# Windowed attention with sinks and channel mix: the sinks' v rows by GpSimd transfers, sink scores of two units in one group, casts off GpSimd, and new instruction orders

## The chip, the cores and the metric

The kernel runs on one core of one Trainium2 chip. The metric is the device time of one execution in microseconds, the median of a few runs. The core's engines are named as the profile names them: PE (matrix multiply), PEld (its weight loads), DVE (vector), ACT (scalar, activations), POOL (GpSimd) and SP (the queue that issues most DMAs).

## The reference, cut to what matters

Attention over 4 batches, 8 heads, 768 positions and a head size of 64, in which a position sees the 128 latest positions and the first four (the sinks); then a channel mix (FFN) over the 512 joined head columns, in which each row is blended with the row before it.

```
keep = (pos[None, :] < n_sink) | ((rel >= 0) & (rel < window))   # n_sink 4, window 128
scores = np.where(keep, scale * q @ k.T, -1e9)
a = exp(scores - max);  a = a / (sum(a) + 1e-9)
x = (a @ v) as [batch, seq, 512]
x_prev = x one position later, zeros first
xk = mu_k * x + (1 - mu_k) * x_prev
xr = mu_r * x + (1 - mu_r) * x_prev
k = maximum(xk @ w_k, 0)                 # 512 -> 1024
v = (k * k) @ w_v                        # 1024 -> 512
out = sigmoid(xr @ w_r) * v
```

## The kernel before

**Tiles.** The 768 positions of a batch are cut into three *units* of 256 positions, 12 units in all, numbered `u`; batch `b, T = divmod(u, 3)`. A unit is taken through four stages, each written as a function that records operations:

- `load` and `prepare(u)`: k, q and v come by SP's DMAs in fp32 (`ks`, `qs`, `vs`, two transfers of 256 KB each, lines 307, 317 and 337). They are cast to bf16 (`kb`, `qb`, `vb`; lines 536, 543, 646) by ACT, DVE or POOL. k and q are turned so that the head dimension lies on the partitions: for early units by PE transposes (L576) and a copy out of PSUM (`kt`, `qt`; L589), for later ones by a DMA transpose (L562).
- `attend(u)`: scores `sc` in PSUM (L721; two heads side by side, each in 64 rows of the PE array: *row-tiled*), `e = exp(sc)` on ACT (L775), a 0/1 mask on DVE (L789; units 0 and 1 have instead a bias that PE adds to the scores, L728, made by POOL in a tile that the profile calls `ob`), value matmuls `vb, e` (L808), and division by the sum of weights, which is a 65th column (reciprocal L822, product `x` L825).
- `mix(u)`: x is transposed (PE L849 and a copy L858, or a DMA transpose L869), the difference with the position before (`td`, L877) and the two blends `xk`, `xr` (L888) are made on DVE.
- `ffn(u)`: keys (L939), relu and square (`rl` L949 or L953, `kk` L963 or L967), gate (L979) with its tanh (`th` L985), product (L997, L909), `(th + 1) * product` on DVE (L1006, L919), store (L1013, L924). The weights `wk`, `wr`, `wv` come in fp32 and are cast once (L501, L505, L507).

**The sinks.** Units with T = 1 and T = 2 do not hold the first four positions of their batch among their own keys, so these come apart. `ksink` holds the four sink keys of all heads (copied by POOL from the turned k of the batch's first unit, L670), `vsink` their value rows. Per unit there is a group of four *column-tiled* matmuls for the sink scores (32 columns each, L696), one `es = exp` on ACT (L703), and sink value matmuls in 64 rows (L763) that start the sums to which L808 adds. `vsink` is made per batch by PE and DVE: a matmul with the 0/1 matrix `spread` puts the four v rows (from `vb` of the batch's first unit) onto the partitions where `es` has their weights, into a PSUM bank (L676); DVE multiplies them there with `hmask`, which keeps a head's rows and clears the others (L680).

**What sets the order.** Nothing is scheduled at run time. The functions record 1,052 operations in a `Plan`; `ORDER` is the list of their numbers in the order in which they are emitted, `CHOICE` says which engine takes an operation that several can do, and `SLOTS` which buffer of a pool each tile gets. Negative entries of `ORDER` are warm matmuls on zeros (L1018), which only keep PE working. Each engine executes its own instructions in this order and waits on semaphores for the others; four PSUM banks (`bank`) and two pairs (`sc`) are shared by all PE work. `JOINT` lists the batches in which the sink scores of the units T = 1 and T = 2 are one group; before, it is empty. Such a batch's third unit is prepared ahead of `attend` of its second (line 1027), since the group needs the q of both.

Of the kernel before, what the change touches and what calls it, by code (L numbers as in the profile page):

```python
# [18 lines left out]
    92: "ACT", 93: "ACT", 94: "ACT", 95: "ACT", 97: "ACT", 100: "ACT", 102: "DVE", 105: "DVE",  # L19
    110: "DVE", 111: "DVE", 114: "ACT", 115: "DVE", 139: "POOL", 142: "POOL", 145: "POOL", 148:  # L20
    "DVE", 150: "DVE", 151: "ACT", 152: "ACT", 154: "DVE", 161: "DVE", 191: "DVE", 193: "DVE",
    194: "DVE", 197: "DVE", 199: "DVE", 200: "DVE", 203: "DVE", 204: "DVE", 213: "DVE", 230:
    "ACT", 234: "ACT", 273: "DVE", 276: "DVE", 279: "DVE", 282: "DVE", 285: "ACT", 286: "ACT",
    298: "DVE", 306: "DVE", 315: "ACT", 354: "DVE", 364: "ACT", 365: "DVE", 367: "DVE", 383:
    "ACT", 387: "ACT", 436: "DVE", 439: "DVE", 444: "DVE", 445: "DVE", 467: "ACT", 475: "ACT",
    514: "DVE", 516: "DVE", 521: "DVE", 524: "ACT", 525: "ACT", 546: "ACT", 550: "ACT", 554:
    "ACT", 558: "ACT", 595: "DVE", 598: "DVE", 603: "ACT", 604: "ACT", 606: "DVE", 634: "ACT",
    681: "DVE", 682: "DVE", 691: "DVE", 700: "ACT", 704: "ACT", 708: "ACT", 755: "DVE", 759:
    "DVE", 760: "ACT", 772: "DVE", 781: "ACT", 785: "ACT", 789: "ACT", 834: "DVE", 836: "DVE",
    837: "DVE", 853: "ACT", 856: "DVE", 857: "ACT", 860: "DVE", 861: "ACT", 904: "DVE", 906:  # L30
    "DVE", 910: "DVE", 912: "DVE", 913: "DVE", 929: "ACT", 933: "ACT", 940: "DVE", 941: "ACT",
    994: "DVE", 995: "ACT", 999: "ACT", 1003: "ACT", 1007: "ACT", 1022: "DVE", 1026: "DVE",
    1034: "DVE", 1035: "ACT",
# [13 lines left out]
JOINT = ()  # L47
# [138 lines left out]
def kernel(  # L186
# [19 lines left out]
    NS = 4  # L206
# [199 lines left out]
    def fill_later():  # L406
        for t in ksink + vsink:
            nc.vector.memset(t, 0.0)
# [666 lines left out]
```

## Time and profile before

| what | value |
|---|---|
| timed runs | 165.51, 165.54 and 166.27 us, median 165.54 us |
| profiled execution, first to last instruction | 164.3 us |
| PE busy / DVE busy / ACT busy / POOL busy | 158.4 / 145.4 / 131.2 / 13.5 us |
| weight loads (PEld) busy | 102.6 us |
| matmuls | 1603 |
| moved by DMA | 34.60 MB, a mean of 211 GB/s |
| HBM read / written | 24.12 / 6.29 MB |
| mean granted TensorE clock | 0.999 |

The profile is of one execution; of its time only the span from the first to the last instruction is known, 164.3 us. How to read its rows: a group of instructions stands with its line, engine, operation, what it writes and reads (`out<-in`, buffer numbers left out), its count, its busy time in us and the mean of one in ns, then the idle time of the engine just before it and who ended it. The windows give, for each stretch, the busy time of each engine. The list of waits says who waited for whom, in us, how often, and the longest. The chain follows the last instruction back to what released it, step by step. Busy times count overlapping instructions of one engine once; the mean of one instruction reaches into the next, so steps of the chain are shorter than the means.

### The profile page before, as it was taken

Reading aid. Unit: us, or ns where it says so; the run is one execution under the profiler, and the core shown is the slowest. Engines: PE = TensorE matmul, PEld = TensorE weight load, DVE = VectorE, ACT = ScalarE, POOL = GpSimd, SP = SyncE. Lnnn points to the kernel's source line nnn. Section 1 sums busy time; section 2 is a strip of 40 time slices with the busy share of each in tenths; the row PEclk is TensorE's granted clock in tenths of the full one; section 3 lists DMA queues with packets and bytes.
Section 4 is the critical chain, followed back from the end, with each engine's and each line's share of the span. In section 5 each row is a group of like instructions: output and inputs, shape, how many; then the busy total and the mean of one; then the engine's idle time right before and its main releaser. Section 6 shows DMA issues by size and latency. Waiting matters only on the chain.

```text
span 164.3 us, 4195 instructions
## 1 busy us (share of the span) xinstructions
PE 158.4 (96%) x1603; PEld 102.6 (62%) x1603; DVE 145.4 (89%) x381; ACT 131.2 (80%) x218; POOL 13.5 (8%) x38
## 2 busy tenths in 40 slices
PE   6999889999999999999999999999999999999992
PEld 2455568866467587577566775856575765664851
DVE  5259999999999999989999999999999999789752
ACT  3277999999999999999999999997668759163240
POOL 6409300010000000060000000000000000000000
PEclk9999999999999999999999999999999999999999
DMA  4999999999969896999999887986996955077743
GB/s 120 247 305 311 348 335 355 301 354 210 228 154 270 135 240 148 234 198 167 224 216 157 188 156 163 235 146 150 199 123 136 362 149 200 0 90 297 262 185 128
DMA packets 79042, 34.60 MB, mean 211 GB/s; under 512 B 67112, under 2 KB 73520, under 8 KB 79024
## 3 DMA queue, kind: packets, MB, share of 16 engines
q1 hardware_dynamic: 79008, 34.35, 86.3%
q8 instruction: 12, 0.20, 0.6%
q14 instruction: 6, 0.05, 0.1%
q10 hardware_dynamic: 16, 0.00, 0.0%
HBM read 24.12 MB, written 6.29 MB: 185 GB/s over the span
## 4 chain that ended last, share of the span: by engine, by line
PE 79%; ACT 8%; SPq 4%; DMA 3%; issue 2%; DVE 1%; POOL 1%; DVEq 0%; ACTq 0%; POOLq 0%
PE bank L997 23%; PE bank L939 23%; PE bank L979 12%; PE bank L808 6%; PE sc L721 6%; SPq L337 3%; DMA qs<-in_q_dram 3%; PE bank L576 2%; ACT e L775 2%; PE bank L849 2%; ACT rl L949 1%; PE bank L763 1%; ACT qt L589 1%; PE bank L909 1%; PE bank L1018 1%
## 5 line engine op out<-in xcount | busy, mean ns | idle before, releaser
L775 ACT ACTIVATE e<-sc 128x1024 bf16<-128x1024 f32 (+1 forms) x48 | 46.1, 994 | 1.8 <-PE sc L721 1.7
L939 PE MATMUL bank<-xk,wk_sb 128*128 128x256 bf16 x384 | 47.1, 273 | 0.0
L997 PE MATMUL bank<-wv_h,kk 128*128 128x512 bf16 x184 | 43.1, 379 | 0.1
L939 PEld LDWEIGHTS <-wk_sb 128*128 128x128 bf16 x384 | 36.4, 98 | 7.4 <-issue 0.4
L949 ACT ACTIVATE rl<-bank 128x512 bf16<-128x512 f32 x40 | 24.2, 625 | 8.6 <-PE bank L939 7.1
L997 PEld LDWEIGHTS <-kk 128*128 128x128 bf16 x184 | 17.1, 98 | 17.8 <-issue 0.4
L789 DVE TENSOR_TENSOR e<-e,mask 128x1024 bf16<-128x1024 bf16 (+1 forms) x40 | 25.4, 642 | 0.7 <-ACT e L775 0.5
L979 PE MATMUL bank<-wr_sb,xr 128*128 128x512 bf16 x96 | 23.7, 379 | 0.0
L888 DVE SCALAR_TENSOR_TENSOR xk<-td,mu_all,xt 128x256 bf16<-128x256 bf16 x48 | 22.4, 483 | 0.3
L888 DVE SCALAR_TENSOR_TENSOR xr<-td,mu_all,xt 128x256 bf16<-128x256 bf16 x48 | 22.1, 475 | 0.2
L967 ACT ACTIVATE kk<-rl 128x512 bf16<-128x512 bf16 x29 | 18.3, 664 | 4.2 <-DVE rl L953 4.0
L985 ACT ACTIVATE th<-bank 128x512 f32<-128x512 f32 x24 | 15.1, 646 | 5.7 <-PE bank L979 5.7
L825 DVE TENSOR_TENSOR x<-bank,rec 128x256 bf16<-128x256 f32 x48 | 19.2, 416 | 0.4
L808 PE MATMUL bank<-vb,e 128*128 128x65 bf16 x352 | 16.6, 194 | 0.0
L1006 DVE SCALAR_TENSOR_TENSOR w<-th,bank 128x512 f32<-128x512 f32 x19 | 13.0, 682 | 3.6 <-issue 1.8
L808 PEld LDWEIGHTS <-e 128*128 128x128 bf16 x352 | 13.6, 97 | 3.5
L979 PEld LDWEIGHTS <-xr 128*128 128x128 bf16 x96 | 8.8, 98 | 8.6 <-issue 0.2
L721 PE MATMUL sc<-qt,kt 64*128 64x128 bf16 (+1 forms) x256 | 13.9, 238 | 0.0
L721 PEld LDWEIGHTS <-kt 64*128 64x128 bf16 x256 | 8.9, 94 | 5.7 <-issue 3.1
L1018 PE MATMUL bank<-warm 128*128 128x512 bf16 x30 | 10.6, 484 | 1.1 <-DVE warm L1038 1.1
L877 DVE TENSOR_TENSOR td<-xt 128x512 bf16<-128x512 bf16 x24 | 10.3, 428 | 0.7 <-ACT xt L858 0.5
L589 ACT COPY qt<-bank 128x512 bf16<-128x512 bf16 x15 | 9.4, 643 | 1.0 <-PE bank L576 1.0
(74 smaller groups left out, 161.7 us busy)
## 6 DMA issues: line engine op xcount, KB each, us to landing
ks<-in_k_dram SPq DMA_DIRECT2D x24, 256.0 KB, 4.7
qs<-in_q_dram SPq DMA_DIRECT2D x24, 256.0 KB, 4.4
vs<-in_v_dram SPq DMA_DIRECT2D x24, 256.0 KB, 4.4
out_dram<-w SPq DMA_DIRECT2D x19, 256.0 KB, 2.7
w<-in_moe_w_k_dram SPq DMA_DIRECT2D x2, 1024.0 KB, 10.4
w<-in_moe_w_v_dram SPq DMA_DIRECT2D x2, 1024.0 KB, 9.3
w<-in_moe_w_r_dram SPq DMA_DIRECT2D x1, 1024.0 KB, 9.7
out_dram<-ob SPq DMA_DIRECT2D x4, 256.0 KB, 2.6
```

The source lines that it names most:

```text
L721: nc.tensor.matmul(out=sc[:, a, o0:o1], lhsT=lhs[rows], rhs=rhs[rows], start=u not in BIAS, stop=True, skip_group_check=u in BIAS)
L775: nc.scalar.activation(out=buf[ek][:, :, lo:], in_=buf[sck][:, :, lo:], func=AF.Exp, scale=scale)
L789: nc.vector.tensor_tensor(out=at, in0=at, in1=m, op=ALU.mult)
L808: nc.tensor.matmul(out=o[:, g, a, :], lhsT=e[:, a, e0:e0 + 128], rhs=rhs, start=(T == 0 and i == 0), stop=(i == len(blocks) - 1), skip_gro ...
L825: P.op("DVE", dve(256), lambda ok=ok, rk=rk, c=c: nc.vector.tensor_tensor(out=buf["x", u][:, :, 128 * c:128 * c + 128].rearrange("p g (a d ...
L888: nc.vector.scalar_tensor_tensor(out=buf[key][:, c, :], in0=buf[tk][:, i, :], scalar=mu[w][:, c:c + 1], in1=xt[:, c, t0 - 1:t0 + 255], op0 ...
L939: nc.tensor.matmul(out=ps[:, i, :], lhsT=wk_sb[:, c, 128 * f:128 * f + 128], rhs=xk[:, c, :], start=(c == 0), stop=(c == NC - 1), skip_gro ...
L949: nc.scalar.activation(out=buf[rk], in_=buf[psk].rearrange("p (i t) -> p i t", i=2), func=AF.Relu)
L967: nc.scalar.activation(out=buf["kk", u][:, 2 * f2:2 * f2 + 2, :], in_=buf[rk], func=AF.Square)
L979: nc.tensor.matmul(out=buf[psk], lhsT=buf["xr", u][:, c, 128 * g:128 * g + 128], rhs=wr_sb[:, c, :], start=(c == 0), stop=(c == NC - 1))
L985: P.op("ACT", act(512), lambda psk=psk, tk=tk: nc.scalar.activation(out=buf[tk], in_=buf[psk], func=AF.Tanh, scale=0.5), rank + 4 + g, tak ...
L997: nc.tensor.matmul(out=buf[psk], rhs=wv_h[:, f, :], lhsT=buf["kk", u][:, f, 128 * g:128 * g + 128], start=(f == 0), stop=(f == NF - 1))
```

## The change

- The four sink rows of v no longer go through PE. A tile `vstage` (128 partitions, 4 batches, 64 columns, fp32) is cleared by DVE at the start. For each of the four sinks POOL issues one transfer that reads that position's row of every head and batch from HBM into every 16th partition of `vstage` (8 partitions, 4 x 64 values). They are POOL's first DMAs in this kernel; all others stay on SP and ACT.
- `vsink` is now `vstage * hmask`, from SBUF. POOL or DVE can do it; the new `CHOICE` gives all four to DVE. The matmul with `spread`, `spread` itself and the PSUM bank are gone. The partitions where a head's sink weights lie change with it (a step of 16 in place of 4, in `ksink`, `hmask` and `vstage` alike).
- `JOINT` names all four batches: the sink scores of the two units of a batch are one group of eight matmuls, with one `es` of 512 columns in place of two of 256.
- POOL has no casts any more (before: one of `qb`, two of `kb`).
- `ORDER`, `CHOICE` and `SLOTS` are new throughout. Counted in the two programs: on ACT four weight casts fewer (two of `wk`, one `wr`, one `wv`), four `es` fewer and of twice the size, nine `qb` casts more and two `kb` casts fewer, two `vb` casts and two `rl` more; on DVE the counterparts, four weight casts more, eight `qb` and two `vb` casts fewer, four `kb` casts more, two `rl` fewer. PE has 1599 matmuls, 30 of them warm ones as before.

The diff, cut to its core (the tables to a line each):

```diff
 CHOICE = {
-    92: "ACT", 93: "ACT", 94: "ACT", 95: "ACT", 97: "ACT", 100: "ACT", 102: "DVE", 105: "DVE",
+    95: "DVE", 96: "ACT", 97: "DVE", 98: "ACT", 99: "DVE", 100: "DVE", 101: "DVE", 102: "DVE",
...
-JOINT = ()
+JOINT = (0, 1, 2, 3)
...
 ORDER = (
-    80, 81, 78, 82, 87, 83, 84, 77, -1, -2, -3, -4, -1, -2, 90, 0, 1, 79, 102, 108, -2, -3, -4,
+    80, 82, 83, -1, -2, -3, -4, -1, 121, 77, 88, 86, 81, 79, 2, 3, 108, 89, 0, 1, 4, 114, -2, -3,
...
-    spread = tile1([128, 128], BF16, "spread")
...
+    vstage = tile1([128, B, D], FP32, "vstage")
...
-        for t in ksink + vsink:
+        for t in ksink + vsink + [vstage]:
             nc.vector.memset(t, 0.0)
...
             m = hmask[:, a::2, :]
-            keep(m, -4 * a, [[-32, NP], [0, D + 1]], 1, m)
-            keep(m, 3 + 4 * a, [[32, NP], [0, D + 1]], -1, m)
+            keep(m, -16 * a, [[-32, NP], [0, D + 1]], 1, m)
+            keep(m, 3 + 16 * a, [[32, NP], [0, D + 1]], -1, m)
...
+    for i in range(NS):
+        P.op("POOL", 1000.0, lambda i=i: nc.gpsimd.dma_start(
+            out=vstage[i::16], in_=v[:, :, i, :].rearrange("b h d -> h b d")), -50,
+            service=60.0, descs=32, reads=["stage0"], writes=[("vstage", i)])
...
-                nc.gpsimd.tensor_copy(out=kz[rows, :, 4 * a:4 * a + NS],
+                nc.gpsimd.tensor_copy(out=kz[rows, :, 16 * a:16 * a + NS],
                                       in_=first(rows))
...
-        psk = ("vsp", b)
-        P.op("PE", 220.0, lambda: nc.tensor.matmul(
-            out=buf[psk].rearrange("p (h d) -> p h d", h=H), lhsT=spread,
-            rhs=buf["vb", u][:, 0, :, 0:D], start=True, stop=True), rank + 4, lag=PE_LAG,
-            take=[("bank", psk)], hold=[("vb", u)], reads=["spread", ("vb", u, 0)], writes=[psk])
-        P.op("DVE", dve(512), lambda: nc.vector.tensor_tensor(
-            out=vsink[b % 2][:, :, 0:D], op=ALU.mult, in1=hmask[:, :, 0:D],
-            in0=buf[psk].rearrange("p (h d) -> p h d", h=H)), rank + 4, hold=[psk],
-            reads=[psk, "hmask", "sinks"], writes=[("vsink", b % 2)])
+        def sink_values(engine):
+            return lambda: engine.tensor_tensor(
+                out=vsink[b % 2][:, :, 0:D], op=ALU.mult, in1=hmask[:, :, 0:D],
+                in0=vstage[:, b, :].unsqueeze(1).to_broadcast([128, H, D]))
+
+        P.op("POOL", 1250.0, sink_values(nc.gpsimd), rank + 4, port=True,
+             alts={"POOL": (1250.0, sink_values(nc.gpsimd), True),
+                   "DVE": (dve(512), sink_values(nc.vector), True)},
+             reads=[("vstage", i) for i in range(NS)] + ["hmask", "sinks"],
+             writes=[("vsink", b % 2)])
```

The places of the order on which the prediction rests stand in it, as rows of the built programs: the first `vsink` on DVE, SP's first loads, and the start of POOL's queue. There `L` numbers are those of the kernel that is shown; most lines of the changed kernel lie some 10 further on.

More of the change, by code (lines that the diff above doesn't have):

```diff
@@ L18 @@
 CHOICE = {
-    92: "ACT", 93: "ACT", 94: "ACT", 95: "ACT", 97: "ACT", 100: "ACT", 102: "DVE", 105: "DVE",
[L20 to L30, printed above, removed]
@@ L31 @@
-    "DVE", 910: "DVE", 912: "DVE", 913: "DVE", 929: "ACT", 933: "ACT", 940: "DVE", 941: "ACT",
-    994: "DVE", 995: "ACT", 999: "ACT", 1003: "ACT", 1007: "ACT", 1022: "DVE", 1026: "DVE",
-    1034: "DVE", 1035: "ACT",
+    95: "DVE", 96: "ACT", 97: "DVE", 98: "ACT", 99: "DVE", 100: "DVE", 101: "DVE", 102: "DVE",
+    103: "DVE", 104: "DVE", 105: "DVE", 107: "ACT", 108: "ACT", 110: "DVE", 111: "DVE", 113:
+    "ACT", 114: "ACT", 116: "DVE", 117: "DVE", 118: "DVE", 120: "DVE", 141: "DVE", 143: "DVE",
@@ new lines @@
+    144: "DVE", 146: "ACT", 147: "DVE", 149: "ACT", 150: "ACT", 152: "ACT", 153: "DVE", 154:
+    "DVE", 156: "DVE", 163: "DVE", 169: "DVE", 171: "ACT", 172: "DVE", 174: "DVE", 175: "ACT",
+    177: "ACT", 178: "ACT", 180: "ACT", 181: "DVE", 182: "ACT", 208: "ACT", 215: "DVE", 223:
+    "ACT", 224: "DVE", 227: "ACT", 228: "ACT", 231: "ACT", 232: "DVE", 235: "ACT", 236: "ACT",
+    273: "DVE", 275: "ACT", 276: "DVE", 278: "ACT", 279: "DVE", 281: "ACT", 282: "ACT", 284:
+    "ACT", 285: "DVE", 286: "ACT", 288: "DVE", 290: "DVE", 297: "DVE", 305: "ACT", 306: "ACT",
@@ new lines @@
+    309: "ACT", 310: "DVE", 313: "ACT", 314: "ACT", 317: "ACT", 318: "ACT", 353: "ACT", 355:
+    "ACT", 357: "ACT", 358: "DVE", 360: "ACT", 362: "ACT", 363: "ACT", 364: "ACT", 366: "ACT",
+    373: "ACT", 381: "ACT", 382: "DVE", 385: "ACT", 386: "ACT", 389: "ACT", 390: "DVE", 393:
+    "ACT", 394: "ACT", 407: "DVE", 409: "DVE", 411: "ACT", 412: "DVE", 414: "ACT", 416: "ACT",
+    417: "ACT", 418: "ACT", 446: "DVE", 453: "ACT", 461: "ACT", 462: "ACT", 465: "ACT", 466:
+    "DVE", 469: "ACT", 470: "ACT", 473: "ACT", 474: "ACT", 511: "DVE", 513: "ACT", 515: "ACT",
@@ new lines @@
+    516: "DVE", 518: "DVE", 520: "ACT", 521: "DVE", 522: "ACT", 524: "DVE", 526: "ACT", 533:
+    "ACT", 541: "DVE", 542: "ACT", 545: "ACT", 546: "ACT", 549: "ACT", 550: "DVE", 553: "ACT",
+    554: "DVE", 589: "DVE", 591: "ACT", 593: "ACT", 594: "DVE", 596: "DVE", 598: "ACT", 599:
+    "ACT", 600: "DVE", 602: "ACT", 609: "ACT", 617: "ACT", 618: "ACT", 621: "ACT", 622: "DVE",
+    625: "ACT", 626: "DVE", 629: "DVE", 630: "DVE", 643: "ACT", 645: "ACT", 647: "ACT", 649:
+    "ACT", 651: "DVE", 652: "DVE", 680: "ACT", 687: "DVE", 695: "ACT", 696: "ACT", 699: "ACT",
@@ new lines @@
+    700: "ACT", 703: "ACT", 704: "ACT", 707: "ACT", 708: "ACT", 745: "ACT", 747: "ACT", 749:
+    "ACT", 751: "ACT", 753: "ACT", 754: "DVE", 756: "DVE", 758: "ACT", 765: "DVE", 773: "ACT",
+    774: "ACT", 777: "ACT", 778: "ACT", 781: "ACT", 782: "ACT", 785: "ACT", 786: "ACT", 821:
+    "ACT", 823: "ACT", 825: "ACT", 827: "ACT", 829: "ACT", 830: "ACT", 845: "ACT", 846: "DVE",
+    849: "ACT", 850: "DVE", 853: "ACT", 854: "ACT", 857: "DVE", 858: "DVE", 871: "ACT", 873:
+    "ACT", 875: "DVE", 877: "ACT", 879: "ACT", 880: "ACT", 921: "ACT", 922: "ACT", 925: "ACT",
@@ L34 @@
+    926: "DVE", 929: "ACT", 930: "ACT", 933: "DVE", 934: "DVE", 985: "ACT", 986: "ACT", 989:
+    "ACT", 990: "DVE", 993: "ACT", 994: "ACT", 997: "ACT", 998: "ACT", 1013: "ACT", 1014: "DVE",
+    1017: "DVE", 1018: "ACT", 1021: "ACT", 1022: "ACT", 1025: "DVE", 1026: "DVE",
 }
@@ L400, in fill @@
     def fill():
-        for t, value in ((ones, 1.0), (spread, 0.0), (hmask, 1.0)):
+        for t, value in ((ones, 1.0), (hmask, 1.0)):
             nc.vector.memset(t, value)
@@ L414 @@
     const_op("DVE", 500.0, fill, ["ones0"], rank=-80)
-    const_op("DVE", 1800.0, fill_later, ["sinks0", "ones", "edges"], rank=-79)
+    const_op("DVE", 1800.0, fill_later, ["sinks0", "stage0", "ones", "edges"], rank=-79)
     def keep(out, base, pattern, multiplier, in_=ones, fill=0.0):
@@ L446, in make_bias1 @@
         window_mask(early.bitcast(BF16)[:, 384:640], warm[:, 0:128], LOW)
-    def make_spread():
-        for a in range(2):
-            nc.gpsimd.tensor_copy(
-                out=spread[0:NS, :].rearrange("p (c w) -> p c w", w=32)[:, :, 4 * a:4 * a + NS],
-                in_=ident[0:NS, 0:NS].unsqueeze(1).to_broadcast([NS, NP, NS]))
     def make_hmask():
@@ L479 @@
     const_op("POOL", 1250.0, make_mask0, ["mask0"], ["ones0"], rank=-55)
-    const_op("POOL", 200.0, make_spread, ["spread"], ["ident", "ones0"], rank=-54)
     const_op("POOL", 1400.0, make_hmask, ["hmask"], ["ones0"], rank=-53)
```

155 rows, old and new, of tables (ORDER, SLOTS) are left out of this document.

## The prediction

> **What bounds the kernel now.** I read the page's busy shares and slices first, then the windows by stage, then the waits, then the chain.
>
> ```profile
> span 164.3 us, 4195 instructions
> PE 158.4 (96%) x1603; PEld 102.6 (62%) x1603; DVE 145.4 (89%) x381; ACT 131.2 (80%) x218; POOL 13.5 (8%) x38
> ...
> PE   6999889999999999999999999999999999999992
> ...
> DVE  5259999999999999989999999999999999789752
> ACT  3277999999999999999999999997668759163240
> ...
> GB/s 120 247 305 311 348 335 355 301 354 210 228 154 270 135 240 148 234 198 167 224 216 157 188 156 163 235 146 150 199 123 136 362 149 200 0 90 297 262 185 128
> ...
> PE 79%; ACT 8%; SPq 4%; DMA 3%; issue 2%; DVE 1%; POOL 1%; DVEq 0%; ACTq 0%; POOLq 0%
> ```
>
> PE is busy in 96% of the span and carries 79% of the chain that ended last. A busy PE is not proof of a full PE, so the windows have to say in which stage something else could hold it (columns: PE, PEld, DVE, ACT and POOL busy, clock, DMA share, GB/s).
>
> ```profile
> 20.00:30.00 10.00, 9.50 (x132) 7.47 (x129) 9.83 (x28) 10.00 (x15) 0.00 (x0) 1.00 1.11 342
> ...
> 60.00:70.00 10.00, 10.00 (x109) 7.01 (x106) 9.71 (x26) 10.00 (x18) 0.00 (x0) 1.00 0.89 194
> ...
> 100.00:110.00 10.00, 10.00 (x121) 6.76 (x119) 9.66 (x26) 10.00 (x18) 0.00 (x0) 1.00 0.97 177
> 110.00:120.00 10.00, 10.00 (x94) 6.25 (x93) 9.93 (x29) 7.66 (x14) 0.00 (x0) 1.00 1.07 158
> ```
>
> From 20 to 110 us three engines are full at once: PE, ACT at 10.00 of 10 and DVE above 9.6. ACT has room only after 110 us (7.66 of 10). So PE sets the time, but work given to ACT or DVE before 110 us has no idle time to fall into. The waits say where PE still stands still:
>
> ```profile
> POOL qb L543 <- DMA qs<-in_q_dram: 6.7, 1, 6.7
> ...
> PE bank L696 <- ACT qt L589: 0.5, 1, 0.5
> PE bank L576 <- DVE vsink L680: 0.5, 1, 0.5
> PE bank L576 <- POOL qb L543: 0.3, 1, 0.3
> ```
>
> The first row is POOL's own wait for a load; the three of PE, 1.3 us together, all lie in the head of the kernel, the one on POOL at 13.5 us behind that load, the other two in PE's timeline (start, us, what, in brackets the idle time ahead and who ended it):
>
> ```profile
> 18.06 0.38 PE L576 MATMUL bank<-ident,qb 128*128 128x128 bf16 x4 [0.46 <-DVE vsink L680]
> ...
> 21.84 0.29 PE L696 MATMUL bank<-qt,ksink 128*32 128x256 bf16 x4 [0.50 <-ACT qt L589]
> ```
>
> The list of waits has no other of PE but for its very first instruction: after the head PE loses almost nothing to data. The profiled execution has a span of 164.3 us; the median of the timed runs, 165.5 us, is 1.2 us more, which lies outside the first and last instruction and which the change does not touch. I make the sum on the profiled execution and add the 1.2 us.
>
> **The change part by part.** Spread matmuls and mode changes, from the chain (start, us, what):
>
> ```profile
> 16.93 0.23 PE bank L676
> ...
> 38.59 0.35 PE bank L808 x8
> ...
> 39.16 0.24 PE bank L808 x8
> ...
> 60.24 0.59 ACT xt L858
> ...
> 64.64 0.50 ACT kb L536
> ...
> 67.06 0.28 ACT es L703
> ...
> 70.27 0.49 ACT rl L949
> ...
> 72.52 0.50 ACT qt L589
> ```
>
> The matmul with `spread` (L676) takes 0.23 us of PE and there are four, one a batch: taken away, 0.9 us less on the engine that sets the end. The same eight value matmuls (L808) take 0.35 us right behind row-tiled ones and 0.24 us elsewhere: PE pays 0.11 us each time it changes between full, row-tiled (scores, sink values) and column-tiled (sink scores) matmuls. Putting the sink scores of two units in one group halves those groups from eight to four, but I count in the two orders of PE how often its mode changes: 66 times before, 67 now, because more score groups stand apart from their sink values. So this part gives PE nothing, +0.1 us. All other matmuls are the same in number and size, the 30 warm ones included.
>
> The vector product for `vsink` moves from PSUM to the staged rows. On DVE, at the first batch, before and then after (names are tiles, `bank` is PSUM):
>
> ```order
> L822 RECIPROCAL rec_104<-bank_65 128x4
> L680 TENSOR_TENSOR vsink_153<-bank_64,hmask 128x8x64
> L825 TENSOR_TENSOR x_107<-bank_65,rec_104 128x2x128
> L543 CAST qb_84<-qs_72 128x2x4x64
> L888 SCALAR_TENSOR_TENSOR xr_117<-td_110,mu_all,xt_155 128x256
> ```
>
> ```order
> L869 COPY xt_155<-bank_64 128x2x256
> L599 COPY qt_91<-bank_66 128x2x256
> L686 TENSOR_TENSOR vsink_152<-vstage,hmask 128x8x64
> L888 TENSOR_TENSOR td_111<-xt_155 128x512
> L656 CAST vb_136<-vs_74 128x8x64
> ```
>
> Before, the product held `bank_64`, which PE's next transposes needed; that is PE's wait of 0.5 us on `vsink`. Now no bank is held, so I take that 0.5 us off. Its cost could lie anywhere between a cast's 0.42 us and a weight cast's 0.68 us (rows below); I leave it as it was, the same operation on as many elements.
>
> SP's loads of the first three units, before and after (`ks_67`, `qs_70` are unit 0's, `ks_68`, `qs_71`, `vs_74` unit 1's, `qs_72`, `ks_69` unit 2's):
>
> ```order
> L307 DMA vs_73<-in_v_dram 128x8x64 x2
> L337 DMA ks_68<-in_k_dram 64x4x256
> L337 DMA qs_71<-in_q_dram 64x4x256 x2
> L337 DMA ks_68<-in_k_dram 64x4x256
> L307 DMA vs_74<-in_v_dram 128x8x64
> L337 DMA qs_72<-in_q_dram 64x4x256 x2
> ```
>
> ```order
> L319 DMA vs_73<-in_v_dram 128x8x64 x2
> L349 DMA ks_68<-in_k_dram 64x4x256 x2
> L349 DMA qs_71<-in_q_dram 64x4x256 x2
> L349 DMA qs_72<-in_q_dram 64x4x256 x2
> L349 DMA ks_69<-in_k_dram 64x4x256 x2
> L319 DMA vs_74<-in_v_dram 128x8x64 x2
> ```
>
> The bytes ahead of the weights are the same, but unit 1's q moves one transfer of 256 KB back, 0.8 us at the 305 to 348 GB/s of those slices. Its cast leaves POOL:
>
> ```profile
> 5.65 0.32 POOL L451 COPY spread<-ident 4x16 bf16<-4x16 bf16 x2
> ...
> 12.64 0.86 POOL L543 CAST qb<-qs 128x512 bf16<-128x512 f32 x1 [6.67 <-DMA qs<-in_q_dram]
> ...
> 13.48 0.62 POOL L543 CAST kb<-ks 128x512 bf16<-128x512 f32 x1
> ...
> 14.05 1.00 POOL L418 TENSOR_SCALAR_AFFINE_SELECT mask<-ones 128x128 bf16<-128x128 bf16 x2
> ...
> 15.07 1.03 PE L728 MATMUL sc<-ob,ident 128*128 128x512 bf16 x4
> ...
> 15.74 0.55 POOL L470 COPY vsink<-hmask 128x8 bf16<-128x8 bf16 x2
> ```
>
> The cast took 0.86 us on POOL. On DVE it takes 0.42 (row below), so 0.4 of the 0.8 us comes back and PE's wait of 0.3 us on that q stays; the third wait, 0.5 us for ACT's `qt` ahead of sink scores, I halve, since the joint group now stands behind both score groups but needs unit 2's q too. What is late next in the head is that q. Head: 0.5 + 0 + 0.25 = 0.75 us less; 0 to 1.3 are the bounds.
>
> What ACT and DVE get is counted from the two orders and priced by the groups (mean ns of one):
>
> ```profile
> L949 ACT ACTIVATE rl<-bank 128x512 bf16<-128x512 f32 x40 | 24.2, 625 | 8.6 <-PE bank L939 7.1 <-ACT kk L967 0.9 <-ACT rl L949 0.2
> ...
> L536 ACT CAST kb<-ks 128x512 bf16<-128x512 f32 x10 | 6.6, 655 | 0.0
> ...
> L543 DVE CAST qb<-qs 128x512 bf16<-128x512 f32 x11 | 4.6, 416 | 2.3 <-DMA qs<-in_q_dram 2.3
> ...
> L501 ACT ACTIVATE wk_sb<-w 128x1024 bf16<-128x1024 f32 x4 | 4.2, 1092 | 0.0
> ...
> L703 ACT ACTIVATE es<-bank 128x256 bf16<-128x256 f32 x8 | 3.3, 407 | 0.0
> ...
> L953 DVE TENSOR_SCALAR rl<-bank 128x512 bf16<-128x512 f32 x8 | 5.5, 685 | 1.5 <-PE bank L939 1.5
> ...
> L543 ACT CAST qb<-qs 128x512 bf16<-128x512 f32 x4 | 2.7, 768 | 0.0
> ...
> L507 DVE CAST wr_sb<-w 128x1024 bf16<-128x1024 f32 x1 | 0.7, 682 | 0.0
> ```
>
> ACT: eight `es` of 0.41 become four of the size of `rl`, 0.63 (-0.8 us); four weight casts go (-4.4); two more `rl` (+1.25); six more `qb` casts at L543 (+4.6) and three more of `qb`, `kb` and `vb` in sum (+2.0): +2.7 us. Means overlap their successors; by the chain's steps (0.50 for a cast, 0.49 `rl`, 0.28 `es`, and 0.95 for a weight cast, its mean less the same 0.14) it is -0.3 - 3.8 + 1.0 + 4.5 = +1.4 us. DVE: six casts fewer (-2.5), four weight casts more (+2.7), two `rl` fewer (-1.4), a memset of `vstage` in its idle head (+0.3): -0.9 us. DVE's relief is behind a full PE and I count it as nothing. ACT's +1.4 to +2.7 us is hidden where PE has FFN matmuls to run; where ACT carries the chain (8% of the span, 13 us, nearly all of it between the first and the last of the chain's ACT rows above, 60 to 73 us) it is not. 13 of the 90 full microseconds is 15%, 0.2 to 0.4 us, and I take 0.5 us to leave something for waits of the new order that no row can show.
>
> POOL's queue, from its masks on, before and after (`ob` is the bias that PE adds to units 0 and 1, its first three rows and memset for unit 0, the next two for unit 1):
>
> ```order
> L418 AFFINE_SELECT hmask<-hmask 128x4x65 x4
> L418 AFFINE_SELECT ob_134<-warm 128x128 x3
> L434 MEMSET ob_134 4x256
> L418 AFFINE_SELECT ob_134<-warm 128x128 x2
> L451 COPY spread<-ident 4x4x4 x2
> L543 CAST qb_83<-qs_71 128x2x4x64
> ```
>
> ```order
> L431 AFFINE_SELECT hmask<-hmask 128x4x65 x4
> L491 DMA vstage<-in_v_dram 8x4x64 x3
> L476 COPY vsink_152<-hmask 128x8
> L476 COPY vsink_153<-hmask 128x8
> L491 DMA vstage<-in_v_dram 8x4x64
> L431 AFFINE_SELECT ob_134<-warm 128x128 x2
> ```
>
> Four transfers now stand ahead of unit 1's bias. Before, `hmask` and both biases were done at 5.65 us; now the window mask (1.00), the `vsink` copies (0.55) and four transfers come first, so the bias is ready at 7.2 us plus four times what a transfer holds POOL. PE used it at 15.07 us. If it is wanted then again, a transfer may take 1.97 us. No row shows a transfer on POOL. The nearest below is a POOL cast, 0.62 to 0.86 us; the nearest above is the landing of an SP store, if POOL were held until then:
>
> ```profile
> out_dram<-w SPq DMA_DIRECT2D x19, 256.0 KB, 2.7
> ```
>
> I take 0.9 us, near the POOL rows, because an issue is an instruction of the queue and not a landing: ready at 10.8 us, nothing lost. The range keeps both ends: 0 and, at 2.7 us each, 18.0 us, 2.9 us late. The longer of the two POOL casts ran beside a DVE cast from 12.62 us on, the shorter one later. The Trainium skill, "SBUF — State Buffer", section "SBUF: two separate sides", says why that could be: GpSimd and some DVE instructions, fp32 copies among them, take an exclusive lock on a shared port pair, and a transfer issued from GpSimd then waits since its descriptors can't be written. The trace agrees as far as 0.62 against 0.86 us goes; the page's own example, some 3.1 us for a transfer beside a DVE copy, would as an estimate put the bias at 19.6 us, 4.5 us late.
>
> The sum: 165.5 - 0.9 + 0.1 - 0.75 + 0.5 = 164.5 us.
>
> **The rivals.** First, the forecast: PE stays full, the four matmuls and about half of the head's waits are saved; 164.5 us, its own range 163.2 (all 1.3 us and a little of DVE's relief) to 164.9. Chance 0.50.
>
> Second, the head gives its part back: unit 2's q and k must now be cast, transposed and copied before the joint sink scores, on an ACT that is full from 20 us on, and unit 1's v comes four transfers later (3.3 us). The three waits then go to other places in the same head, and new ones take half of what the four matmuls gave: 165.5 - 0.9 + 0.1 + 0.5 = 165.2 us. For it speaks that ACT's `qt` copy ended one of the waits already; against it that fewer casts stand between load and transpose. Chance 0.26.
>
> Third, on the other side: ACT becomes the bound. Its extra work lies before 110 us, where its windows read 10.00 of 10, and PE runs out of FFN matmuls as it did between 60 and 73 us. It decides from about 2.4 us of unhidden ACT work on; at the full 2.7 us: 165.5 - 0.9 + 0.1 - 0.75 + 2.7 = 166.7 us. Against it: only 13 us of the chain are ACT's, and it can catch up after 110 us. Chance 0.14.
>
> Fourth, POOL: the transfers hold it for more than 1.97 us each, PE waits for the bias of unit 1, and with a full PE behind it all of that stays. At 2.7 us each: 164.5 + 2.9 = 167.4 us. For it: the 0.86 us cast beside DVE. Against it: a third of the 1.97 us is what POOL's casts take at their quickest. Chance 0.10.
>
> **How the numbers follow.** 164.5 us is the likeliest. A measurement of this kernel can tell about 0.5% (0.8 us) from no change, so faster means below 164.7 and slower above 166.4 us. Most of the forecast's 0.50 lies below 164.7 and a little of it not: faster 0.48. The rest of it, the second case and the mild half of what ACT could cost: same 0.30. ACT at its full price and POOL: slower 0.22. The range, 163.2 to 166.6 us, holds the first two cases and the milder part of the third; outside are POOL (0.10), ACT at its worst (0.06) and a little below.
>
> **What would show it.** Right: the wait of PE's transposes on `vsink` gone; PE's busy time lower by about 1 us, with ACT still at 10.00 of 10 between 20 and 110 us; POOL done with unit 1's bias near 11 us. Wrong: a PE wait on POOL `ob` near 15 us (fourth case); ACT with a share of the chain well over 8% (third); PE waits in the head that still sum to more than 1 us (second).

## The result, and the profile after

The changed kernel took 166.83 us (median of 16 runs, 165.78 to 168.5), the kernel before, timed beside it, 165.91 us (median of 16, 165.51 to 166.85). The ratio is 1.0052, with a 95% interval of 1.0028 to 1.0075: slower by half a per cent, where 164.5 us and a gain had been forecast. In a second measurement it was 1.0074 (1.0047 to 1.0101). Averages below leave out the few executions that lay over 1.5% above their kernel's fastest, three of the changed kernel's 27 among them (with these three its mean span is 165.08 us).

Each run lists its time and its span, first to last instruction. Over all runs of the study:

| | runs | mean span, us | spread of the spans (standard deviation) | time less span |
|---|---|---|---|---|
| before | 99 | 164.34 ± 0.04 | 0.41 | 1.86 |
| after | 24 | 164.92 ± 0.14 | 0.69 | 2.12 |

The changed kernel was measured ahead of the experiments and beside the first set of them, not beside the later two; before, measured beside each of the three sets, has mean spans of 164.23, 164.39 and 164.30 us, so a difference of 0.1 or 0.2 us between sets says nothing.

The loss of 0.84 us has two parts: 0.26 us outside the span and 0.58 us in it, together with a wider spread. The profiled execution of the changed kernel shows nothing of the second part: at 163.7 us it is the fastest of its 24. Its page (the first line of part 1, two DMA queues of part 3, the chain's shares):

```profile
span 163.7 us, 4180 instructions
PE 157.6 (96%) x1599; PEld 101.6 (62%) x1599; DVE 144.6 (88%) x377; ACT 132.5 (81%) x221; POOL 10.8 (7%) x37
...
q1 hardware_dynamic: 79008, 34.35, 91.1%
...
q0 software_dynamic: 128, 0.03, 0.1%
...
PE 84%; ACT 5%; DVE 3%; DMA 3%; issue 1%; SPq 1%; DVEq 0%; ACTq 0%
```

PE's busy time fell by 0.8 us (158.4 before) and ACT's rose by 1.3 (131.2). The queue of software transfers, q0, is new: the 128 packets that GpSimd starts. PE's list of waits, whole:

```profile
PE bank L1029 <- DVE warm L1049: 1.1, 1, 1.1
PE bank L586 <- ACT qb L553: 0.5, 1, 0.5
PE bank L774 <- ACT es L714: 0.4, 1, 0.4
PE sc L732 <- ACT kt L599: 0.2, 1, 0.2
PE sc L732 <- ACT e L786: 0.2, 1, 0.2
```

The first row is the very first instruction, as before. The wait on `vsink` is gone, and so are the other two; four others stand in their place, and their sum is 1.3 us as it was. The windows over the head and over the stretch from there to 160 us, of before and then of after (PE, PEld, DVE, ACT, POOL busy, clock, DMA share, GB/s):

```profile
0.00:24.00 24.00, 21.48 (x217) 11.69 (x218) 16.75 (x54) 16.31 (x26) 9.86 (x32) 1.00 0.94 277
24.00:160.00 136.00, 135.85 (x1380) 90.20 (x1380) 127.65 (x326) 114.88 (x193) 3.62 (x6) 1.00 0.87 202
```

```profile
0.00:24.00 24.00, 21.30 (x227) 11.63 (x228) 18.22 (x57) 16.41 (x26) 9.32 (x31) 1.00 0.96 276
24.00:160.00 136.00, 135.80 (x1374) 89.78 (x1371) 125.79 (x319) 116.05 (x197) 1.52 (x6) 1.00 0.93 203
```

Between 24 and 160 us PE is full in both. In the head PE stands idle for 2.5 us before and 2.7 us after. Two of its new waits, in its timeline:

```profile
6.00 0.62 PE L586 MATMUL bank<-ident,qb 128*128 128x128 bf16 x8 [0.47 <-ACT qb L553]
...
21.48 0.29 PE L774 MATMUL bank<-vsink,es 64*128 64x130 bf16 x4 [0.36 <-ACT es L714]
```

The first stands ahead of unit 0's transposes: both halves of unit 0's q are now cast by ACT, one behind the other (4.80 and 5.33 us), where before the two halves of the first load, k, were cast side by side on ACT and DVE (4.84 and 4.86 us). The second is the wait for the joint `es`. POOL's queue, which one rival feared:

```profile
5.41 1.76 POOL L491 DMA_DIRECT2D vstage<-in_v_dram  x3
7.17 0.36 POOL L476 COPY vsink<-hmask 128x8 bf16<-128x8 bf16 x2
7.43 0.70 POOL L491 DMA_DIRECT2D vstage<-in_v_dram  x1
8.14 0.72 POOL L431 TENSOR_SCALAR_AFFINE_SELECT ob<-warm 128x128 bf16<-128x128 bf16 x2
```

A transfer holds POOL for 0.6 to 0.7 us here, and the bias of unit 1 is done at 8.9 us.

### The profile page after: what moved, and what is told of

The parts are those of the page before. It is cut to its first block, busy times and chain, and to the rows that moved or that the text cites. A ratio compares the mean times of both kernels' runs of the same rounds, so it can differ in the third digit from the quotient of the medians.

```text
span 163.7 us, 4180 instructions
## 1 busy us (share of the span) xinstructions
PE 157.6 (96%) x1599; PEld 101.6 (62%) x1599; DVE 144.6 (88%) x377; ACT 132.5 (81%) x221; POOL 10.8 (7%) x37
## 4 chain that ended last, share of the span: by engine, by line
PE 84%; ACT 5%; DVE 3%; DMA 3%; issue 1%; SPq 1%; DVEq 0%; ACTq 0%
PE bank L950 26%; PE bank L1008 24%; PE bank L990 13%; PE bank L819 7%; PE sc L732 6%; DMA ks<-in_k_dram 3%; ACT e L786 3%; PE bank L860 2%; PE bank L586 2%; PE bank L774 2%; SPq L349 1%; PE bank L920 1%; DVE x L836 1%; ACT kt L599 1%; PE bank L707 1%
## 5 line engine op out<-in xcount | busy, mean ns | idle before, releaser
L786 ACT ACTIVATE e<-sc 128x1024 bf16<-128x1024 f32 (+1 forms) x48 | 45.5, 970 | 1.8 <-PE sc L732 1.7
L950 PE MATMUL bank<-xk,wk_sb 128*128 128x256 bf16 x384 | 46.4, 273 | 0.0
L1008 PE MATMUL bank<-wv_h,kk 128*128 128x512 bf16 x184 | 44.0, 379 | 0.0
L960 ACT ACTIVATE rl<-bank 128x512 bf16<-128x512 f32 x42 | 24.8, 613 | 10.9 <-PE bank L950 10.8
L1008 PEld LDWEIGHTS <-kk 128*128 128x128 bf16 x184 | 17.1, 98 | 16.8
L899 DVE SCALAR_TENSOR_TENSOR xk<-td,mu_all,xt 128x256 bf16<-128x256 bf16 x48 | 21.7, 478 | 0.0
L996 ACT ACTIVATE th<-bank 128x512 f32<-128x512 f32 x24 | 14.5, 614 | 4.3 <-PE bank L990 3.9
L888 DVE TENSOR_TENSOR td<-xt 128x512 bf16<-128x512 bf16 x24 | 9.8, 417 | 1.6 <-DMA xt<-x 1.6
L1029 PE MATMUL bank<-warm 128*128 128x512 bf16 x30 | 9.6, 427 | 1.1 <-DVE warm L1049 1.1
L833 DVE RECIPROCAL rec<-bank 128x4 f32<-128x4 f32 x48 | 7.8, 174 | 2.0 <-PE bank L819 1.5
```

What stands on the lines that cost most here:

```text
L786: nc.scalar.activation(out=buf[ek][:, :, lo:], in_=buf[sck][:, :, lo:], func=AF.Exp, scale=scale)
L899: nc.vector.scalar_tensor_tensor(out=buf[key][:, c, :], in0=buf[tk][:, i, :], scalar=mu[w][:, c:c + 1], in1=xt[:, c, t0 - 1:t0 + 255], op0 ...
L950: nc.tensor.matmul(out=ps[:, i, :], lhsT=wk_sb[:, c, 128 * f:128 * f + 128], rhs=xk[:, c, :], start=(c == 0), stop=(c == NC - 1), skip_gro ...
L960: nc.scalar.activation(out=buf[rk], in_=buf[psk].rearrange("p (i t) -> p i t", i=2), func=AF.Relu)
L996: P.op("ACT", act(512), lambda psk=psk, tk=tk: nc.scalar.activation(out=buf[tk], in_=buf[psk], func=AF.Tanh, scale=0.5), rank + 4 + g, tak ...
L1008: nc.tensor.matmul(out=buf[psk], rhs=wv_h[:, f, :], lhsT=buf["kk", u][:, f, 128 * g:128 * g + 128], start=(f == 0), stop=(f == NF - 1))
```

## The experiments

**The transfers.** The first theory (A) was that transfers started by GpSimd cost time outside the span. The rivals: the order itself is slower (B), or the transfers disturb the span (C). Four kernels; the first is the changed kernel unaltered.

> The changed kernel once more, for its profile, its spans and a second set of times. The theory (A): the transfers that GpSimd starts itself cost a fixed time ahead of the first or behind the last instruction, so the run's time is again about 2.1 us longer than its span, where before's is 1.2 us longer. The rival (B): the new order is itself slower or more easily disturbed, so that the span, 163.7 us in the first profile, comes out near before's 164.3 or above. The other rival (C): the four transfers disturb other transfers inside the span, in some executions more than in others; then the span varies by over 1 us and the wait rows of VectorE, ScalarE or TensorE on DMAs do so with it.

Measured: 167.44 us (median of 11), mean span 165.17, 2.14 us outside it.

```
-        P.op("POOL", 1000.0, lambda i=i: nc.gpsimd.dma_start(
+        P.op("POOL", 1000.0, lambda i=i: nc.scalar.dma_start(
```

> The changed kernel, with the four transfers into vstage started by ScalarE's queue in place of GpSimd's; nothing else differs. Theory A: the time outside the span falls from 2.1 us to about 1.2, and the kernel runs in about 165.9 us where the changed one takes 166.8, against 165.9 before: 0.995 of the changed kernel. Rival B: no difference to the changed kernel over 0.3 us, and 2.1 us outside the span stays. Rival C: the time outside stays at 2.1 us, and the span varies less from run to run.

Measured: 167.97 us, 1.0105 of before (1.0075 to 1.0134); outside the span 1.73 us, a fall as A has it, though of 0.4 us and not of 0.9, and a mean span of 166.1 us. Set against the first profile of the changed kernel, its profile is 1.4 us late at 24 us and 2.4 us at the end, so more than half of what it loses lies in the head. There ACT issues the transfers between its casts, and SP, which waits for earlier loads to land as well (1.8 us for `ks`), now waits for one of these too (SP's waits, then ACT's timeline):

```profile
SPq L349 <- DMA vstage<-in_v_dram: 1.5, 1, 1.5
```

```profile
4.85 0.69 ACTq L491 DMA_DIRECT2D vstage<-in_v_dram  x1
5.58 0.62 ACT L553 CAST qb<-qs 128x512 bf16<-128x512 f32 x1
5.59 1.27 ACTq L491 DMA_DIRECT2D vstage<-in_v_dram  x2
```

```
-        P.op("POOL", 1000.0, lambda i=i: nc.gpsimd.dma_start(
-            out=vstage[i::16], in_=v[:, :, i, :].rearrange("b h d -> h b d")), -50,
+        P.op("POOL", 1000.0, lambda: None, -50,
```

> The changed kernel without the four transfers into vstage: the sinks' v rows stay zero, so the sinks' part of the numerator is left out of the output; every other instruction is there. Theory A: about 1.2 us outside the span and about 165.9 us in all, as with the transfers started by ScalarE. Rival B: as slow as the changed kernel, 166.8 us. Rival C: the span is shorter in its slower runs than the changed kernel's, with 2.1 us outside.

Measured: 166.66 us, 1.0038 of before (1.0015 to 1.0061); outside the span 1.70 us, mean span 164.99 ± 0.20. The span is no shorter without the transfers (C falls), and half of the loss or more stays without them: 1.0038 of before, where the changed kernel has 1.0074 beside it and 1.0052 in the first measurement (B, in part).

In the next kernel these lines stand at the end of `make_spread`, where GpSimd is idle:

```
+        for i in range(NS):
+            nc.gpsimd.dma_start(out=vstage[i::16], in_=v[:, :, i, :].rearrange("b h d -> h b d"))
```

> The kernel before, with the four transfers added on GpSimd's queue at a place where GpSimd stands idle (6 to 12.6 us); the tile that they fill is read by nothing, and nothing waits for them. Theory A: the span stays at 164.3 us, the time outside it rises from 1.2 to about 2.1 us, and the kernel takes about 0.85 us longer than before, a ratio of 1.005. Rival B: the ratio is 1.000 within 0.002, since the order is before's. Rival C: the span itself grows by some tenths of a us, and its runs spread more than before's.

Measured: 166.53 us, 1.0025 of before (1.0008 to 1.0042); outside the span 2.08 us instead of 1.86, mean span 164.53 ± 0.17 instead of 164.34. A later run of the same with `range(1)`:

> The kernel before with one of the four transfers on GpSimd's queue (the other three left out), its tile read by nothing. With four the time outside the span rose from 1.87 to 2.08 us. If that is a price of the program (it has such transfers or has none) it comes to 2.08 again; if it is a price of each transfer, to 1.92.

Measured: 1.98 us outside the span, ratio 1.0006 (0.9986 to 1.0026). So one transfer costs 0.12 us outside the span and four cost 0.22: neither a price of the program alone nor an equal one of each. A is right, and small: about a quarter of a microsecond of the loss. In the new order the same four transfers are worth 0.42 us (2.12 against 1.70); that order without them has 0.16 us less outside the span than before has, and no run shows why. (The 1.2 us that I call before's time outside the span in these expectations, and 1.9 later, are the same thing; the 1.2 was wrong, see below.)

**Where long executions lose.** The kernel without transfers happened to be profiled in a span of 166.6 us, 2.9 us over the first profile of the changed kernel, with the same instructions in the same order but for those four. Set against that profile, PE's k-th weight load is level at 6 us, 0.8 us late at 23 us, 1.4 at 48 and, within a few matmuls at 90 us, 3.0 us late; then nothing more is lost. PE waits there on ACT. The same stretch of ACT's timeline, first in the fast profile of the changed kernel, then in the long one:

```profile
83.11 0.59 ACT L599 COPY qt<-bank 128x512 bf16<-128x512 bf16 x1 [0.18 <-PE bank L586]
83.59 1.14 ACT L546 CAST kb<-ks 128x512 bf16<-128x512 f32 x2
84.63 1.94 ACT L786 ACTIVATE e<-sc 128x1024 bf16<-128x1024 f32 x2
```

```profile
84.53 0.59 ACT L598 COPY qt<-bank 128x512 bf16<-128x512 bf16 x1 [0.18 <-PE bank L585]
85.02 0.62 ACT L545 CAST kb<-ks 128x512 bf16<-128x512 f32 x1
87.49 0.62 ACT L545 CAST kb<-ks 128x512 bf16<-128x512 f32 x1 [1.85 <-DMA ks<-in_k_dram]
88.02 1.93 ACT L785 ACTIVATE e<-sc 128x1024 bf16<-128x1024 f32 x2
```

The chain of the long execution runs through this load, from its issue on (start, us, what):

```profile
82.80 4.67 DMA ks<-in_k_dram
87.47 0.02 issue
87.49 0.03 ACT kb L545
```

The second half of unit 8's k landed late, the cast waited 1.85 us for it, and behind it on ACT's queue stood the exponentials that PE needed. In the fast profile that load landed 0.25 us ahead of its cast. The other places are of the same kind: DVE's cast of `wr_sb` waits in the long profile, and a cast of `qs` at 100 us waits in the fast one (first the long, then the fast). That last wait, 1.17 us long, cost PE next to nothing: PE had matmuls of the product (L1008) to run meanwhile. What a late load costs depends on what stands behind its cast.

```profile
37.13 1.29 DVE L516 CAST wr_sb<-w 128x1024 bf16<-128x1024 f32 x2 [0.98 <-DMA w<-in_moe_w_r_dram]
```

```profile
35.46 1.29 DVE L517 CAST wr_sb<-w 128x1024 bf16<-128x1024 f32 x2
...
99.98 0.62 ACT L546 CAST qb<-qs 128x512 bf16<-128x512 f32 x1 [1.17 <-DMA qs<-in_q_dram]
```

I then counted in the traces, for each load past 24 us whose landing is recorded (46 or 47), how long before its read it landed. Under 0.5 us: none of before's and one in a second profile of it; eight to ten in three profiles of the new order, nine in the first. (The counts in the next expectation, six and one, were made before each piece was matched with its own cast.) Hence theory D: the new order lets loads land just in time; against it E: it loses in the head or on the engines.

The lines for v; those for k and q that SP turns are cut in the same way, with `n = 8 if g else 128`:

```
-                        out=buf[key][:, g, :, :],
-                        in_=v[b, :, s0:s0 + 128, :].rearrange("h p d -> p h d")), rank,
+                        out=buf[key][0:n, g, :, :],
+                        in_=v[b, :, s0:s0 + n, :].rearrange("h p d -> p h d")), rank,
...
+                    n = 8 if g and u >= 3 else 128
```

> So far: the span of the changed kernel has a mean of 165.1 us over 27 runs (163.7 to 166.4), that of the kernel before 164.2 over 27 (163.5 to 165.2); without the four transfers it is 165.2, so they are not what lengthens it. In a long execution the engines wait for loads that land late: ScalarE 1.9 us for ks at 87.5 us. New theory (D): the new order lets more loads land just before they are read (past 20 us six within 0.5 us of their cast, in the kernel before one), so that a transfer that is late delays the in-order ScalarE or VectorE and then TensorE. Here the second piece of every v load from unit 3 on, and of every k and q load that SP turns, fetches 8 of its 128 rows; the rows of the sequence that they leave out keep older numbers, so the output is not the reference's. Every instruction stays. D: with these loads landing early, the mean span falls by 0.5 us or more, to 164.5 or less, and the long executions over 165.5 go. Rival E (the new order loses its time in the head, before 24 us, or on the engines themselves): the span stays at 165.1 within 0.3 and varies as before.

Measured: mean span 164.03 ± 0.15, 0.9 us less; 165.97 us in all, 0.9993 of before (0.9968 to 1.0017). As D has it.

> The kernel before with the same loads thinned in the same way (8 of 128 rows in the second piece of v from unit 3 on and of each k and q load that SP turns; the output is not the reference's). D: next to nothing is gained, since these loads land 2 us or more ahead of their casts: mean span 164.2 within 0.2. E: the same, 164.2. If it falls by as much as the changed kernel does, then the loads bound both kernels alike, and D is not what tells them apart.

Measured: mean span 164.67 ± 0.16, no gain; 1.0023 of before (1.0000 to 1.0046). So 0.9 us of the new order's span, and nothing of the old one's, hangs on these loads. Thinning takes away traffic as well as lateness; that lateness is enough, the run with every load whole shows below.

> The changed kernel with the second pieces of the k loads of units 8 and 9 issued ahead of the two turns of q of unit 8 on SP's queue, about 1.3 and 3.3 us sooner. Nothing else is moved. D: the 0.25 and 0.40 us between these pieces' landing and their casts become over 1 us, the wait of ScalarE at 87 us in long executions goes, and the mean span falls by 0.1 to 0.4 us. E: no change, 165.1 within 0.2.

Measured: mean span 164.84 ± 0.17, 1.0048 of before (1.0022 to 1.0075). Not to be told from the changed kernel: two of the places are not enough. The wait at 87 us, the largest loss in the long profile, is thus not all that sets the mean.

> The kernel before unchanged, for a second profile of it and its own spread: ratio 1.000 within 0.001, span 164.2 on the mean with all runs within 163.4 and 165.3, time outside the span 1.87 us.

Measured: 166.27 us, 1.0017 (0.9991 to 1.0042), mean span 164.51 ± 0.17, one run at 166.0. The span and the spread are a little more than expected, the time outside, 1.87 us, as expected. Set against the first profile of before, PE's weight loads differ by up to 0.8 us until 20 us and from 22 us on by a constant 0.15 us, to the end. In three more profiles (before with one or four transfers added, and with the thinned loads) the lag past 23 us is constant to within 0.03 us too, at 0.20, 1.54 and 1.31 us: in these profiles the old order loses and gains in its head alone.

**The order of the loads.** SP's queue, the rows that move (ordinary text, tiles with their buffers; `w322` holds w_r, `ks0` and `qs0` unit 3's k and q, then the second pieces of k of units 8 and 9 ahead of the turns of unit 8's q; the second piece of unit 9's q, not shown, goes behind its first):

```
+DMA w322<-in_moe_w_r_dram
 DMA ks0<-in_k_dram
 DMA qs0<-in_q_dram x2
 DMA ks0<-in_k_dram
-DMA w322<-in_moe_w_r_dram
...
+DMA ks2<-in_k_dram
+DMA ks0<-in_k_dram
 DMA_TRANSPOSE qt0<-qb2
-DMA ks2<-in_k_dram
 DMA_TRANSPOSE qt0<-qb2
 DMA_TRANSPOSE kt0<-kb2
 DMA vs2<-in_v_dram
-DMA ks0<-in_k_dram
```

> The changed kernel with four loads issued earlier on SP's queue: w_r ahead of the loads of k and q of unit 3 (27.5 to about 21 us), the second piece of q of unit 9 right behind its first (94.8 to about 90.7), and the second pieces of k of units 8 and 9 as in the run before. Every load is whole. D: the late landings at 35 (w_r), 84 to 89 (k) and 100 us (q) go; the mean span falls from 165.1 to 164.4 or less, towards the 164.0 of the thinned loads, and nothing past 24 us differs between executions by over 0.3 us; the time comes to 166.3 or 166.5, level with before within 0.3 per cent, the 0.24 us outside the span being still there. E: no change, 165.1 and 167.1.

Measured: 166.15 us, 1.0002 of before (0.9984 to 1.0019), mean span 164.07 ± 0.10, standard deviation 0.33 where the changed kernel has 0.69. All of the 0.9 us of the thinned loads is back with every load whole, and past 24 us the lag of PE's weight loads against the fast profile stays between 0.48 and 0.60 us. Against the run with two pieces sooner (164.84 us) only w_r and the piece of unit 9's q are new, so most of the gain hangs on these two; no run parts them. A load that lands late is not harmful as such: this profile still has about six loads that land within 0.5 us of their reads, two of which are waited for (0.17 us at 111 us on ACT, 0.23 us at 114 us on DVE), and PE loses nothing there. In the window from 20 to 30 us (columns as above), in the changed kernel and then in this one, the loads have moved forward; before has 342 GB/s in its row:

```profile
20.00:30.00 10.00, 9.36 (x133) 6.59 (x132) 9.68 (x28) 9.80 (x15) 0.00 (x0) 1.00 0.98 283
```

```profile
20.00:30.00 10.00, 9.18 (x137) 6.32 (x134) 9.78 (x28) 9.59 (x14) 0.00 (x0) 1.00 1.06 332
```

The reverse, in the kernel before:

```
 DMA ks0<-in_k_dram x2
-DMA w322<-in_moe_w_r_dram
 DMA vs2<-in_v_dram
 DMA qs0<-in_q_dram x2
+DMA w322<-in_moe_w_r_dram
```

> The kernel before with one load later on SP's queue: w_r behind the second piece of v of unit 2 and the two pieces of q of unit 3 (21.7 to about 26.6 us). In its profile w_r landed at 31.4 us and ScalarE read it at 32.3. D: it lands 1 to 3 us late, ScalarE waits for it, and the mean span rises from 164.35 by 0.6 to 1.6 us. E: the order of the loads does not matter, 164.35 within 0.3.

Measured: 167.32 us, 1.009 of before (1.0051 to 1.0129), mean span 165.84 ± 0.34, 1.5 us more and a standard deviation of 0.95. Its profile was taken in its mildest execution, a span of 165.0 us, and has the wait at the place (before, then this kernel):

```profile
32.26 1.18 ACT L501 ACTIVATE wr_sb<-w 128x1024 bf16<-128x1024 f32 x1
```

```profile
33.17 1.06 ACT L499 ACTIVATE wr_sb<-w 128x1024 bf16<-128x1024 f32 x1 [0.41 <-DMA w<-in_moe_w_r_dram]
```

Of the 1.5 us this profile shows 0.5: PE's lag against the first profile of before steps from 0.27 to 0.79 us behind the wait and then stays. Two of the eight executions, of 167.2 and 167.4 us, had a granted clock of 0.990, the others 0.997 or more; without these two the mean span is 165.35 us, 1.0 us more than before. How the longer executions lose the rest no profile shows. One load, moved by three places in a queue, costs the old order at least as much as the whole change did. D holds in both directions.

No version beat both kernels: the one with four loads earlier is level with before, its span 0.27 us shorter and its time outside 0.24 us longer.

## Why the prediction was wrong, point by point

**"1.2 us more, which lies outside the first and last instruction and which the change does not touch".** This step failed twice. The 1.2 us was the median of three timed runs less the span of another execution; where time and span of one run are both known, 1.86 us lie outside. And the change does touch it: +0.26 us. That GpSimd's transfers add to it is shown by adding them to before (+0.22 us), by their removal (2.12 to 1.70 us) and by ACT starting them (1.73); why the two orders differ by 0.16 us without them stays open. The base of 165.5 us was low as well: the median of 16 runs of before was 165.91.

**Spread matmuls and mode changes, -0.9 + 0.1.** Right: PE's busy time is 0.8 us less.

**The head, -0.75.** Wrong: the `vsink` wait went, as said, but PE's head waits sum to 1.3 us again and its idle time in the first 24 us is 2.7 us instead of 2.5. The head gives its part back, as the second rival had it, and the text named 1 us as the sign of that; but only the wait for the joint `es` (0.4 us) comes the way that the rival describes. The longest, 0.5 us, is for ACT's cast of unit 0's q at 6.0 us, which neither the forecast nor a rival looked at.

**ACT, +0.5, and its price in bounds of +1.4 to +2.7 us of work.** The work came out at +1.3 us, just under the lower bound. It cost PE nothing in the profiled execution: PE is busy for 135.80 of 136 us past the head, against 135.85. The third rival's sign, a share of the chain well over 8%, did not come (5%).

**POOL.** The transfers took 0.6 to 0.7 us, less than the 0.9 I took, and unit 1's bias was ready at 8.9 us instead of 10.8; the fourth rival is out. The Trainium skill, "SBUF — State Buffer", section "SBUF: two separate sides", tells of some 3.1 us for a transfer beside a DVE copy; these four did not show it, though the last of them (7.43 us, 0.70 us) ran beside two casts on DVE from 7.54 us on.

**What no term held: the loads, +0.9 us on the mean.** This is the step that failed most: after the head the forecast let PE lose nothing to loads. All that it set aside for new waits was the part of ACT's 0.5 us "to leave something for waits of the new order that no row can show", 0.1 to 0.3 us. SP's new order was read for the first three units only, where it changed the order of the bytes. Past them w_r is issued at 27.5 us where before issued it at 21.7, and nine loads land within half a microsecond of their reads. That ACT and DVE were full I took as a price of added work alone; it also means that neither has room to wait, so a late load can go through to PE, as at 87 us in the long execution. The profile of before could not show it, since there every load past 24 us had 0.8 us or more, but its traffic row (342 GB/s between 20 and 30 us) and the new order on SP could have asked the question.

The sum, worked again with what was measured: base 165.9; PE and head together -0.3 (thinned loads against before, 164.03 to 164.34); late loads +0.9; outside the span +0.26: 166.8 us, against 166.83 measured. The terms are differences between these same runs, so that they add up is bookkeeping and no test. The -0.3 is a mean over executions; the two profiles have -0.6, of single ones. How much of the difference is the head's, where profiles of the old order differ from its first by up to 1.5 us, the runs do not settle, nor why a load lands later in one execution than in another.

## What to carry to other kernels

When an order changes, compare for every load how long it lands ahead of its read, not only what stands in the engines' queues: in-order engines that are full can pass a late load on to the bound engine, namely where what that engine needs next stands behind the load's reader, and the time grows with the spread of the landings, which one profile, the fastest above all, does not show. Take the time outside the span from the same execution as the span. A wider spread of a kernel's runs is itself a finding: line the traces of a short and a long execution up instruction by instruction and see where the lag steps.

## What the runs showed of the hardware

- Transfers that GpSimd starts cost time that lies in no instruction: 0.12 us for one and 0.22 us for four, added to before; 0.42 us for the four when taken from the changed kernel. Started by ACT they cost nothing outside the span (1.73 us against 1.70 without any).
- Such a transfer of 8 KB held POOL for 0.54 to 0.77 us in seven profiles (several in a row by their mean), and landed 3.7 to 4.2 us after its issue (medians).
- Four profiles of the old order repeat its first past the head to 0.03 us in PE's timeline, and differ from it by up to 1.5 us at 23 us. The exception is the one with w_r issued later.
- Fetching 8 of 128 rows in some of its loads gave the kernel before no gain (1.0023, 1.0000 to 1.0046), and a mean span 0.3 us longer, not shorter.
